# A 480-byte tile at the far end of the right side of SBUF, ahead of every other tile there

## The chip, the cores and the metric

The kernel runs on one core of one Trainium2 chip. The metric is the device time in microseconds of one execution. A profile of one execution of the kernel before is there as well; its "span" runs from the first to the last instruction on the core.

## The reference

Three layers run one after the other, all in float32, on 1,536 tokens (2 batches of 768) of width 512:

```
attention: 8 heads of 64; each query sees the keys less than 16 positions away,
           and 24 block summaries (max of k, mean of v over 32 tokens)
moe:       a token with x @ w_skip > 0 is computed, the others pass;
           its expert e = argmax(x @ w_gate) of 8;  x += gate * relu(x @ w1[e]) @ w2[e]
           w1 is 8 x 512 x 1024, w2 is 8 x 1024 x 512
moe2:      out = (sigmoid(x @ w_gate) * (x @ w_val)) @ w_out,   512 -> 1536 -> 512, float64 weights
```

The third layer's weights arrive as 64-bit words; the kernel makes float32 values of them and splits each into a high part of type fp32r, on which TensorE runs in one pass, and a low part that holds the rest.

## The kernel before

**Stages.** Attention fills the first 80 us: 12 tiles of 128 tokens, whose operations stand in an order that a planner worked out ahead from written costs. Each tile's result goes to a DRAM tile x_d. The MoE stage runs to about 200 us: 64 tiles of weights (512 KB each) and four tiles of raw weights of the third layer stream in through three rings of buffers, SP issuing every load; eight experts run one after the other on TensorE (`e_s1` L731, `e_s2_mm` L764, plain float32). POOL gathers tokens from x_d by index (L709, L1010) and adds results back into x_d by index (L787, L895). These adds and gathers follow one another, since each waits for the one that last wrote x_d. For experts with many tokens `o_tile` runs a second tile with split weights (`mm`, L860). In this execution it ran twice. The rest, from about 200 us, is the third layer.

**The third layer.** d_ff = 1536 is cut into six groups g of 256 columns, the tokens into three parts c of 512. A unit u = 3g + c does for one group and one part:

- `m_s1(u, f)` for f = 0, 1: for gate and value, four blocks n of the width, three matmuls each, 24 in all, 48 in a unit (L1175);
- `m_gate`: sigmoid on ACT, product on DVE, its high part on ACT, its low part on DVE (L1187 to L1191);
- `m_s2(u - 1, r)` for r = 0 to 3, one unit later: six matmuls each, 24 in all (L1204), and the sum in ACC on DVE (L1210, L1212).

```
for a, b in ((hi, XH), (hi, XL), (lo, XH)):
    x = b[c][n] if c == 0 else b[c][:, n, :]
    pe.matmul(ps, a[:, o:o + 128], x, start=k == 0, stop=k == 11)        # L1175: stationary, moving
...
for a, b in ((GH, hi), (GH, lo), (GL, hi)):
    pe.matmul(ps, a[u][:, f, r * 128:r * 128 + 128], b[:, o + a0:o + a1], ...)   # L1204
```

Here hi, lo = WHL[g % 2]. `m2_split` makes the weights of a group out of raw ones (L983 to L997, on DVE, ACT and POOL) while earlier units run. The first two units are broken by transposes of the tokens, `x2` (L1153), which wait for loads of x_d (L1148).

**Where the tiles lie.** A pool stands on the left or on the right side of SBUF. Left pools grow up from the low addresses, right ones down from byte 229,344 of a partition, which is 447 x 512 + 480. The sizes of the pools' large tiles are multiples of 512 bytes. The addresses that the program has before, in bytes of a partition:

| side | tile | first byte | past a multiple of 512 |
|---|---|---|---|
| left | XH[0], XL[0] (eight of 2 KB) and `o_tile`'s split weights | 19,968 to 36,352 | 0 |
| left | WHL[0]: wh0, wl0 | 36,352; 48,640 | 0 |
| left | ring b (loads 25 to 34 of the weights) | 36,352 to 77,312 | 0 |
| right | `o_tile`'s split tokens xoT, hoT | 90,976 to 99,168 | 352 |
| right | xgT, the MoE stage's tokens | 105,312; 107,360 | 352 |
| right | GH, GL (two of each) | 122,848; 126,944; 131,040; 135,136 | 480 |
| right | ACC | 147,424 | 480 |
| right | WHL[1]: wh1, wl1 | 172,000; 184,288 | 480 |
| right | XH[1], XH[2], XL[1], XL[2] | 196,576; 204,768; 212,960; 221,152 | 480 |
| right | rings a and c (the other weights, the raw ones) | 131,040 to 229,344 | 480 |

So in L1175 the stationary operand is left for even g and right for odd g, the moving one left for c = 0 and right for c = 1, 2. In L1204 the stationary operand (GH, GL) is always right and the moving one left for even g, right for odd g. In L860 the stationary operand (xoT, hoT) is right, at 352, the moving one left, at 0.

Of the kernel before, what the change touches and what calls it, by code (L numbers as in the profile page):

```python
# [9 lines left out]
F32 = mybir.dt.float32  # L10
# [141 lines left out]
def body(ctx: ExitStack, tc, qx, kx, vx, vtx, cst, csa, wgs, w1, w2, mgate, mval, mout, out):  # L152
    nc = tc.nc
    pe, dve, act, pool, sp = nc.tensor, nc.vector, nc.scalar, nc.gpsimd, nc.sync
# [20 lines left out]
    MORE = keep.tile([128, E, 12], F32, name="MORE")  # L175
    WIDX = keep.tile([128, NOV], I32, name="WIDX")
    NL = keep.tile([128, 1], I32, name="NL")

    wst = ExitStack()
    wring = wst.enter_context(tc.tile_pool(name="wring", bufs=NWA, side="right"))  # L180
# [266 lines left out]
    def count():  # L447
# [6 lines left out]
        dve.tensor_reduce(NLF, MORE.rearrange("p a b -> p (a b)"), axis=AX, op=ALU.add)  # L454
        dve.tensor_copy(NL, NLF)

# [443 lines left out]
    lp = lst.enter_context(tc.tile_pool(name="lp", bufs=1, side="left"))  # L900
    nl = nc.values_load(NL[0:1, 0:1], min_val=0, max_val=NOV)
    with tc.If(nl > 0):
# [393 lines left out]
```

## Time and profile before

| | |
|---|---|
| median of 3 runs | 512.0 us (511.83 to 513.35) |
| the profiled execution | 514.23 us, span 512.4 us |
| mean granted TensorE clock of the profiled execution | 0.97 of full speed |
| TensorE matmul busy | 491.8 us, 96% of the span |
| VectorE, ScalarE, GpSimd busy | 287.4, 187.3, 108.6 us |
| moved by DMA | 83.08 MB |

A busy time is the time in which an engine had an instruction in flight. Matmuls are pipelined, so the busy time of one is longer than its distance to the next: in the rows below a matmul lasts some 0.39 us and the next starts some 0.23 us after it. The pace is therefore read from a stretch of consecutive matmuls divided by their number.

### The profile page before, as it was taken

What the parts mean: (1) busy time and instruction counts of PE and PEld (TensorE: products, weight loads), DVE (VectorE), ACT (ScalarE), POOL (GpSimd) and SP (SyncE); (2) the same over time, 40 slices, a digit from 0 to 9 for tenths busy, and PEclk for the clock granted to TensorE, in tenths of its full rate; (3) what the DMA queues carried; (4) which work ended last, traced back from release to release, by engine and by line L of the source; (5) the groups of instructions that cost most, each with busy time, mean ns of one, the idle gap of its engine ahead of it and who ended that gap; (6) DMA issues with size and microseconds to landing.
All of it is one profiled execution on the core that took longest, in us unless ns stands there. A gap on an engine that the chain in (4) does not pass through costs nothing.

```text
span 512.4 us, 8115 instructions
## 1 busy us (share of the span) xinstructions
PE 491.8 (96%) x2889; PEld 372.3 (73%) x2889; DVE 287.4 (56%) x813; ACT 187.3 (37%) x403; POOL 108.6 (21%) x157
## 2 busy tenths in 40 slices
PE   6999998899999978899999999999999999999997
PEld 3988884346574535688888888888888888888886
DVE  4889787217481544257855565455646465456324
ACT  2888862017471323234432233223232232222110
POOL 5664223610121221012211121112211221112000
PEclk9799997599999989899999999999999999999999
DMA  8889889999997863742222220122012220000114
GB/s 272 295 247 305 239 285 347 376 349 405 392 399 276 252 202 97 233 187 83 82 82 84 82 83 6 78 82 83 19 64 83 82 83 0 1 0 0 43 41 165
DMA packets 27483, 83.08 MB, mean 162 GB/s; under 512 B 3096, under 2 KB 5016, under 8 KB 25384
## 3 DMA queue, kind: packets, MB, share of 16 engines
q1 hardware_dynamic: 25032, 77.71, 43.1%
q0 software_dynamic: 2400, 4.72, 4.1%
q8 instruction: 28, 0.46, 0.4%
q14 instruction: 23, 0.19, 0.1%
HBM read 73.69 MB, written 8.13 MB: 160 GB/s over the span
## 4 chain that ended last, share of the span: by engine, by line
PE 58%; DMA 8%; issue 2%; SPq 0%; POOLq 0%; DVE 0%
PE s L1175 38%; PE s L1204 19%; DMA x_d<-ysb,SI 6%; PE x2p L1153 1%; DMA xg<-x_d 1%; DMA x2t<-x_d 1%; DMA x_d<-yo,SI 0%; SPq L1100 0%; POOLq L1028 0%; DVE ACC L1212 0%; POOLq L787 0%; SPq L1148 0%; POOLq L997 0%
## 5 line engine op out<-in xcount | busy, mean ns | idle before, releaser
L1175 PE MATMUL s<-XH,wh 128*128 128x512 f32 x288 | 114.1, 396 | 0.0
L1175 PE MATMUL s<-XH,wl 128*128 128x512 f32 x288 | 113.2, 393 | 0.0
L1175 PE MATMUL s<-XL,wh 128*128 128x512 f32 x288 | 113.2, 393 | 0.0
L997 POOL TENSOR_TENSOR wl<-x,wh 128x512 fp32r<-128x512 f32 x32 | 42.1, 1317 | 223.1 <-ACT wh L996 214.4
L1189 DVE TENSOR_TENSOR pr<-s,sg 128x512 f32<-128x512 f32 x36 | 24.9, 691 | 92.6 <-PE s L1175 88.8
L1175 PEld LDWEIGHTS s<-XH,wh 128*128 128x128 f32 x288 | 54.4, 189 | 12.4 <-issue 0.2
L1175 PEld LDWEIGHTS s<-XH,wl 128*128 128x128 f32 x288 | 54.2, 188 | 12.4
L1175 PEld LDWEIGHTS s<-XL,wh 128*128 128x128 f32 x288 | 54.2, 188 | 12.3 <-DVE XL L1128 0.2
L1204 PE MATMUL s<-wh,GL 128*128 128x512 f32 (+1 forms) x146 | 56.8, 389 | 0.0
L1204 PE MATMUL s<-wl,GH 128*128 128x512 f32 (+1 forms) x146 | 56.8, 389 | 0.0
L1204 PE MATMUL s<-wh,GH 128*128 128x512 f32 (+1 forms) x146 | 56.8, 389 | 0.0
L1190 ACT ACTIVATE GH<-pr 128x512 fp32r<-128x512 f32 x36 | 22.8, 632 | 68.0 <-DVE pr L1189 68.0
L996 ACT ACTIVATE wh<-x 128x512 fp32r<-128x512 f32 x36 | 22.7, 632 | 67.2 <-DVE x L990 67.2
L1212 DVE TENSOR_TENSOR ACC<-s,ACC 128x512 f32<-128x512 f32 (+1 forms) x61 | 39.1, 677 | 7.8 <-PE s L1204 7.8
L1191 DVE TENSOR_TENSOR GL<-pr,GH 128x512 fp32r<-128x512 f32 x36 | 24.9, 692 | 25.1 <-ACT GH L1190 25.1
L985 ACT ACTIVATE u<-u 128x512 f32<-128x512 f32 x36 | 22.5, 626 | 43.5 <-DVE u L983 43.5
L731 PE MATMUL hp<-wt,xgT 128*64 128x512 f32 x128 | 33.7, 657 | 0.6 <-ACT xgT L721 0.6
L341 ACT ACTIVATE P<-P,nm 128x120 f32<-128x120 f32 x96 | 29.7, 383 | 5.8 <-DVE nm L334 5.8
L1204 PEld LDWEIGHTS s<-wl,GH 128*128 128x128 f32 x146 | 27.4, 188 | 6.1
L1204 PEld LDWEIGHTS s<-wh,GH 128*128 128x128 f32 x146 | 27.4, 188 | 6.1
L1204 PEld LDWEIGHTS s<-wh,GL 128*128 128x128 f32 x146 | 27.4, 188 | 6.0
L325 PE MATMUL S<-kw,qb 128*128 128x120 f32 x192 | 28.5, 295 | 3.0 <-DVE kw L548 1.8
(185 smaller groups left out, 695.5 us busy)
## 6 DMA issues: line engine op xcount, KB each, us to landing
wt<-w SPq DMA_DIRECT2D x64, 512.0 KB
wr<-mout SPq DMA_DIRECT2D x6, 1024.0 KB
wr<-mgate SPq DMA_DIRECT2D x5, 1024.0 KB
wr<-mval SPq DMA_DIRECT2D x5, 1024.0 KB
vw<-vx SPq DMA_DIRECT2D x12, 390.0 KB
kr<-kx SPq DMA_DIRECT2D x8, 400.0 KB
qs<-qx SPq DMA_DIRECT2D x12, 256.0 KB
vt<-vtx SPq DMA_DIRECT2D x8, 384.0 KB
```

Of the source, the lines that this page charges most:

```text
L325: pe.matmul(Sp[i][:, n, :], qb[t % 3][:, j, n, :], kwb[i % 3][:, n, :], start=True, stop=True)
L341: act.activation(Pt[i][:, n, :], Pt[i][:, n, :], AF.Exp, bias=nmt[i][:, n:n + 1], scale=-1.0)
L731: pe.matmul(hp[e][c * 64:c * 64 + 64, :], xgT[e // 2][:, n, (e % 2) * 64:(e % 2) * 64 + 64], WT[2 * e, n][:, c * 512:c * 512 + 512], start ...
L985: act.activation(u, u, AF.Copy, scale=2.0 ** -112)
L996: act.activation(hi[:, d], w, AF.Copy)
L997: (dve if g == 0 and k < WLE else pool).tensor_tensor(lo[:, d], w, hi[:, d].bitcast(F32), op=ALU.subtract)
L1175: pe.matmul(ps, a[:, o:o + 128], x, start=k == 0, stop=k == 11)
L1189: dve.tensor_tensor(pr, pp[1], sg, op=ALU.mult)
L1190: act.activation(GH[u][:, f, :], pr, AF.Copy)
L1191: dve.tensor_tensor(GL[u][:, f, :], pr, GH[u][:, f, :].bitcast(F32), op=ALU.subtract)
L1204: pe.matmul(ps, a[u][:, f, r * 128:r * 128 + 128], b[:, o + a0:o + a1], start=k == 0, stop=k == 5)
L1212: dve.tensor_tensor(acc, ps, acc, op=ALU.add)
```

## The change

A pool of one tile is opened on the right side before all others there. It is 120 float32 values wide (480 bytes) and stays to the end. POOL clears its first column; nothing reads it. All other tiles of the right side come to lie 480 bytes lower, the left side stays.

```
     NL = keep.tile([128, 1], I32, name="NL")
 
+    edge = ctx.enter_context(tc.tile_pool(name="edge", bufs=1, side="right"))
+    EDGE = edge.tile([128, 120], F32, name="EDGE")
+    pool.memset(EDGE[:, :1], 0.0)
+
     wst = ExitStack()
     wring = wst.enter_context(tc.tile_pool(name="wring", bufs=NWA, side="right"))
```

The right side's large tiles of the third layer and of the rings then stand at 0 past a multiple of 512 (wh1 at 171,520 = 335 x 512), xoT, hoT and xgT at 384. Tiles of attention that stood at an odd multiple of 32 bytes come to an even one, and the other way round.

## Rows read from the trace of the kernel before

**Rows 1.** The page: the span, and busy time by engine.

```profile
span 512.4 us, 8115 instructions
PE 491.8 (96%) x2889; PEld 372.3 (73%) x2889; DVE 287.4 (56%) x813; ACT 187.3 (37%) x403; POOL 108.6 (21%) x157
```

**Rows 2.** Chain that ended last, 212 to 510 us: start, length, what.

```profile
by line: PE s L1175 65.1%; PE s L1204 33.4%; PE x2p L1153 1.2%; DVE ACC L1212 0.1%; issue 0.0%
...
217.01 8.36 PE s L1175 x36
...
229.91 2.80 PE s L1175 x12
232.72 5.60 PE s L1204 x24
238.31 11.20 PE s L1175 x48
...
271.92 10.92 PE s L1175 x48
282.83 5.44 PE s L1204 x24
288.27 10.88 PE s L1175 x48
...
304.60 10.91 PE s L1175 x48
315.51 5.47 PE s L1204 x24
320.99 11.20 PE s L1175 x48
```

**Rows 3.** Windows, L1175 alone: busy, PEclk, DMA share, GB/s.

```profile
255.12:266.31 11.19, 11.19 (x48) 8.65 (x47) 1.00 0.27 94
271.92:282.83 10.91, 10.91 (x48) 8.66 (x47) 1.00 0.19 81
304.60:315.51 10.91, 10.91 (x48) 8.66 (x47) 1.00 0.20 83
320.99:332.18 11.19, 11.19 (x48) 8.67 (x47) 1.00 0.20 83
```

**Rows 4.** Timeline of TensorE in the first o_tile, 119 to 133 us.

```profile
127.48 0.40 PE L860 MATMUL yq<-wh,hoT0l 128*128 128x512 f32 x1
...
132.17 0.39 PE L860 MATMUL yq<-wh,hoT1l 128*128 128x512 f32 x1
```

**Rows 5.** Timeline of POOL, 130 to 212 us: adds into x_d, idle before them.

```profile
133.87 1.59 POOL L895 DMA_INDIRECT x_d<-yo,SI  x1 [11.15 <-DVE yo L894]
142.65 1.67 POOL L787 DMA_INDIRECT x_d<-ysb,SI  x1 [7.20 <-DMA x_d<-yo,SI]
```

**Rows 6.** Chain that ended last, before 212 us.

```profile
166.86 4.30 DMA x_d<-ysb,SI
...
171.91 9.74 DMA x_d<-ysb,SI
...
189.37 3.98 DMA x_d<-ysb,SI
```

**Rows 7.** Timeline of TensorE: L731 with weights right, then left (expert 3).

```profile
113.61 1.94 PE L731 MATMUL hp<-wt,xgT 128*64 128x512 f32 x8
...
134.95 1.94 PE L731 MATMUL hp<-wt,xgT 128*64 128x512 f32 x8
```

**Rows 8.** SP's loads; windows of their stream: busy by engine, PEclk, DMA share, GB/s.

```profile
103.96 30.77 SPq L278 DMA_DIRECT2D wt<-w  x23
135.75 1.53 SPq L278 DMA_DIRECT2D rh<-mgate  x2
...
121.50:126.50 5.00, 4.99 (x24) 3.63 (x22) 4.25 (x8) 4.44 (x9) 1.01 (x1) 1.00 1.02 419
...
142.50:147.30 4.80, 4.80 (x24) 3.87 (x23) 3.78 (x7) 4.15 (x8) 1.67 (x1) 1.00 1.04 422
```

**Rows 9.** Timelines of POOL and TensorE at the start.

```profile
0.33 0.10 POOL L1286 MEMSET const-uint8-127<- 128x1 uint8 x1
0.72 0.52 POOL L530 MEMSET Z<- 128x512 f32 x1 [0.29 <-POOLq L1286]
...
8.15 0.68 PE L325 MATMUL S<-kw,qb 128*128 128x120 f32 x4 [1.01 <-ACT kw L547]
```

**Rows 10.** Window of unit 2: busy on PE, PEld, DVE, ACT, POOL; then POOL's splits.

```profile
238.00:249.50 11.50, 11.50 (x51) 9.27 (x50) 9.79 (x18) 4.06 (x7) 2.32 (x2) 1.00 0.08 13
...
248.47 3.19 POOL L997 TENSOR_TENSOR wl<-x,wh 128x512 fp32r<-128x512 f32 x2 [6.77 <-ACT wh L996]
```

## The prediction

> **What bounds the kernel now.** I read the page first: matmuls are in flight for 96% of the span [rows 1]. The chain of waits then says where that decides. From 212 us to the end the chain is TensorE and nothing else, 65.1% in L1175 and 33.4% in L1204, with no wait between [rows 2]. So in the third layer, nearly 300 of 512 us, the time is the number of matmuls times their pace, and whatever changes the pace comes out at the end in full. Before 212 us the chain is a string of DMAs that add into x_d one after the other [rows 6].
>
> The second reading is the pace itself, from the pieces of that chain. The same 48 matmuls of L1175 take 11.20 us in some units (238.31, 320.99) and 10.88 in others (288.27): 233.3 ns and 226.7 ns each. The 24 of L1204 take 5.60 or 5.44, the same two paces [rows 2]. [...]
>
> What sorts them is where the two operands lie. By the kernel's loop, g is even in units 0 to 2, 6 to 8, 12 to 14:
>
> - L1175, both operands left (unit 6 at 304.60, c = 0, g even): fast. Both right (units 4 and 5 at 271.92 and 288.27): fast.
> - L1175, one left and one right (unit 2 at 238.31, unit 7 at 320.99; unit 3 as well, at 255.12 [rows 3]): slow.
> - L1204, both right (g odd, 282.83): fast; stationary right, moving left (g even, 232.72, 332.18 and seven more): slow.
>
> The units not shown, up to 17, repeat this. Left tiles start at a multiple of 512 bytes, right ones 480 past one. So "one left, one right" is also "the two start 480 bytes apart in that count", and "same side" is "0 apart". After a change of sides the first dozen matmuls still run between the paces, which is why 271.92 has 10.92 and not 10.88 [rows 2].
>
> **The change part by part.** (1) *Third layer.* After the change left and right tiles all start at a multiple of 512. If the distance of the operands sets the pace, every unit has what both-left units have now (0 and 0), which is fast. What goes, from the chain's pieces against 10.88 and 5.44: eight L1175 units of 11.19 to 11.20 (units 2, 3, 7, 8, 9, 13, 14, 15), 8 x 0.32 = 2.53 us with the hundredths; nine L1204 pieces of 5.60, 9 x 0.16 = 1.44; five units of 10.91 and 10.92 and four of 5.45 and 5.47, 0.26 together; units 0 and 1, which transposes break up, 36 matmuls in 8.36 instead of 36 x 0.2267 = 8.16, and two dozens in 2.80 instead of 2.72, 0.36. Sum 4.59 [rows 2]. The four transposes' breaks stay and leave some uneven matmuls behind them; I take 4.5. Bounds: 0 if the side and not the distance is what counts; 4.6 above.
>
> (2) *o_tile.* L860 has its stationary operand at 352 and its moving one at 0. It runs at (132.17 - 127.48) / 20 = 234.5 ns, slow too [rows 4]. This speaks against the mere distance in bytes: these tiles lie 55 to 79 KB from their moving ones and are slow, GH and GL 33 to 74 KB from wh1 and wl1 and fast. After the change it stands at 384 against 0; no row has that distance. If that is as good as 0, some 43 matmuls of the first tile save 0.008 each, 0.33 us. VectorE, which makes the split weights, is busy 4.25 of 5.00 us there [rows 8], so it can follow. The add of this tile's result is issued at 133.87 right after DVE, and the next add, 142.65, waits for it [rows 5]; from there the chain of adds runs to 212 us, so the 0.33 could come through whole. The second tile's saving falls beside that chain and is worth nothing. Bounds 0 to 0.33; I take 0.15, as 384 is unseen.
>
> (3) *Other matmuls.* Plain float32 ones don't show the two paces: L731 takes 1.94 us per eight with weights on the right (expert 2, 128 bytes from xgT) and on the left (expert 3, 352) [rows 7]. So moving the tiles of attention and of the experts costs and gives nothing on TensorE; the cover for a hundredth either way is the chain of adds.
>
> (4) *DMA.* The weight rings a and c come to multiples of 512, ring b is there already. Loads land in order of issue: ring b's, the 25th to 34th, are the 4th to 13th of the 23 issued from 103.96 on, the raw ones, which lie right, are issued from 135.75, and both arrive some 6 us later. The rate is 419 GB/s in a window of the former and 422 in one of the latter [rows 8]. So 0 from this. [...]
>
> (5) *The clear.* One more POOL memset ahead of Z. A one-column memset takes 0.10 us [rows 9]. It shifts the warm-up matmuls, whose end is followed by 1.01 us of waiting for ACT [rows 9]: hidden, and 0.1 us if that cover went.
>
> (6) *What is next.* A unit and its L1204 piece come to 16.32 us. In unit 2 DVE is busy 9.79 of 11.50 us and POOL ends the splits for unit 3 at 251.66 [rows 10], 3.4 us ahead of their use at 255.12 [rows 3]. TensorE is about 1 us earlier by then, so the splits are still in time. DVE has less to do later.
>
> Sum: 4.5 + 0.15 = 4.65 us. The profiled execution had 514.23 us with a span of 512.4; the span would be 507.75. The runs' median is 512.0, 2.2 under the profiled execution's time; the same saving gives 507.35, say 507.4.
>
> **The rivals.** *(B) Nothing changes: 512.0.* The pace goes with the side, by some part of SBUF, and not with the distance modulo 512. For it: before, the two can't be parted in the third layer. Against it: L860, whose distances overlap the fast ones, and that both-left and both-right pairs have one pace to within 1 ns. [...]
>
> *(D) Part of the gain is given back: 508.8.* DVE, 85% busy in unit 2 [rows 10], becomes the bound in units 1 to 3, while it makes the second group's weights. Then their 3 x (0.32 + 0.16) = 1.4 us don't come. Against it: 3.4 us of margin.
>
> *(C) Slower.* TensorE's 0.3 us in the o_tiles move the last weight loads, issued from 168 us on, against the adds into x_d. An add took 9.74 us among those loads and 4.30 or 3.98 outside [rows 6], each on the chain. One more such add costs 5.44: 507.35 + 5.44 = 512.8, still the same; two cost 5.44 + 5.76: 518.5, slower. It decides only from the second on, and needs both of them among the loads.
>
> [...]
>
> **How the numbers follow.** The forecast (all units fast, 506.2 to 508.4) has 0.75, D 0.08, B 0.11, C 0.04 (half of it in each of its two ends), E 0.02. The range 505.9 to 510.0 holds the forecast with repeats and D, and leaves out B, C and E, under 2 in 10. Faster by over 0.3%, about what a measurement of this kernel can tell, means under 510.5: 0.75 + 0.08 + 0.02 = 0.85. Same 0.11 + 0.02 = 0.13; slower 0.02.
>
> **What would show it.** All L1175 pieces of the chain from unit 2 on at 10.88 and all L1204 ones at 5.44, with no second level; L860 at 227 ns or at 234 tells whether 384 counts as 0; L731 at 1.94; the weight stream at 420 GB/s; the add at 133.87 earlier by up to 0.33 us. The prediction is wrong if units with one operand on each side stay at 11.20 (B), if they all go to 11.20, or if 212 us, where the third layer's chain begins, moves by more than a few tenths.

## The result, and the profile after

The changed kernel has a median of 507.17 us (11 runs, 504.0 to 510.82) against 513.35 (11 runs, 509.51 to 514.7) for the kernel before. The ratio is 0.990, interval 0.9869 to 0.9932: faster by 0.7 to 1.3%. A later series of 12 more runs gave 507.68 and a ratio of 0.9916, interval 0.9885 to 0.9947. The profiled execution took 510.82 us, span 509.0 us.

Line numbers from L179 on are four higher than before. The page of the changed kernel, span and busy time, as in [rows 1]:

```profile
span 509.0 us, 8116 instructions
PE 486.7 (96%) x2889; PEld 371.7 (73%) x2889; DVE 287.2 (56%) x813; ACT 187.2 (37%) x403; POOL 107.8 (21%) x158
```

The chain that ended last, changed kernel, third layer, as in [rows 2] (start, length, what):

```profile
211.84 1.90 PE x2p L1157 x8
213.74 3.56 PE s L1179 x12
...
218.17 8.18 PE s L1179 x36
...
230.84 2.74 PE s L1179 x12
233.57 5.44 PE s L1208 x24
239.01 10.88 PE s L1179 x48
...
255.33 10.88 PE s L1179 x48
...
271.65 10.88 PE s L1179 x48
...
320.61 10.88 PE s L1179 x48
331.49 5.44 PE s L1208 x24
...
505.68 0.42 DVE ACC L1216
```

The second level is gone. The units at 239.01 (unit 2, one operand on each side), 255.33 (unit 3, the sides exchanged) and 320.61 (unit 7) now take what unit 4 at 271.65 takes. The piece that had 10.92 at a change of sides has 10.88 as well. The windows say the same at the same clock, 1.00, and with much the same transfers beside them as in [rows 3]:

```profile
255.33:266.21 10.88, 10.88 (x48) 8.67 (x47) 1.00 0.28 96
...
320.61:331.49 10.88, 10.88 (x48) 8.66 (x47) 1.00 0.21 86
```

The end of the chain before, for the sum that follows:

```profile
509.06 0.42 DVE ACC L1212
```

From unit 2's L1175 to the last sum in ACC the profile before has 509.06 - 238.31 = 270.75 us, the one after 505.68 - 239.01 = 266.67: 4.08 less. Units 0 and 1 give 0.18 (36 matmuls, 8.18 instead of 8.36), 0.12 (the two dozens) and 0.16 (the first L1204 piece). Together 4.54 us.

This leaves out the dozen of unit 0 between the first two sets of transposes, at 213.74, whose operands both lie left in both kernels. It took 3.56 us after and 3.32 before, and from the first transposes to the end the third layer is 4.34 us shorter. In 213.40 to 215.30 us of the profile after, the granted clock was 0.50; TensorE had waited 2.28 us for tokens just before. In the traces of the experiments below the dozen takes from 2.74 us (E5) to 4.32 (E7), and the wait alone doesn't set it: before, TensorE had waited longer, 2.44 us, and the dozen was shorter.

The rest of the rows are about what they were. The extra expert tile, timeline of TensorE as in [rows 4]:

```profile
128.41 0.39 PE L864 MATMUL yq<-wh,hoT0l 128*128 128x512 f32 x1
...
133.06 0.40 PE L864 MATMUL yq<-wh,hoT1l 128*128 128x512 f32 x1
```

The adds into x_d, POOL's timeline as in [rows 5], then the chain before 212 us as in [rows 6]:

```profile
134.77 1.59 POOL L899 DMA_INDIRECT x_d<-yo,SI  x1 [11.69 <-DVE yo L898]
```

```profile
168.60 8.05 DMA x_d<-ysb,SI
...
177.39 7.08 DMA x_d<-ysb,SI
...
185.21 4.33 DMA x_d<-ysb,SI
...
190.27 3.83 DMA x_d<-ysb,SI
```

The stream of weights in the two windows of [rows 8], and POOL's start as in [rows 9]:

```profile
121.50:126.50 5.00, 5.00 (x25) 4.10 (x24) 4.00 (x7) 4.39 (x8) 1.00 (x1) 1.00 1.03 420
142.50:147.30 4.80, 4.80 (x22) 3.83 (x21) 3.80 (x7) 3.65 (x8) 1.82 (x1) 1.00 1.03 421
```

```profile
0.72 0.10 POOL L181 MEMSET EDGE<- 128x1 f32 x1 [0.29 <-POOLq L1290]
...
0.76 0.52 POOL L534 MEMSET Z<- 128x512 f32 x1
```

In this profile the third layer starts 0.96 us later than before (211.84 against 210.88) and is 4.34 us shorter, so the spans differ by only 3.4 us. Whether that delay belongs to the change is asked below.

### The profile page after: what moved, and what is told of

Read it like the earlier page. It is cut to its first block, busy times and chain, and to the rows that moved or that the text cites. A ratio compares the mean times of both kernels' runs of the same rounds, so it can differ in the third digit from the quotient of the medians.

```text
span 509.0 us, 8116 instructions
## 1 busy us (share of the span) xinstructions
PE 486.7 (96%) x2889; PEld 371.7 (73%) x2889; DVE 287.2 (56%) x813; ACT 187.2 (37%) x403; POOL 107.8 (21%) x158
## 4 chain that ended last, share of the span: by engine, by line
PE 58%; DMA 8%; issue 2%; SPq 0%; POOLq 0%; DVE 0%
PE s L1179 38%; PE s L1208 19%; DMA x_d<-ysb,SI 6%; PE x2p L1157 1%; DMA xg<-x_d 1%; DMA x2t<-x_d 1%; DMA x_d<-yo,SI 0%; SPq L1104 0%; POOLq L1032 0%; DVE ACC L1216 0%; POOLq L791 0%; SPq L1152 0%; POOLq L1001 0%
## 5 line engine op out<-in xcount | busy, mean ns | idle before, releaser
L1191 ACT ACTIVATE sg<-s 128x512 f32<-128x512 f32 x36 | 21.1, 587 | 26.0 <-PE s L1179 26.0
## 6 DMA issues: line engine op xcount, KB each, us to landing
wt<-w SPq DMA_DIRECT2D x64, 512.0 KB, 11.3
```

Source lines behind the costliest of these rows:

```text
L1191: act.activation(sg, pp[0], AF.Sigmoid)
```

## The experiments

Two theories of the gain stood against each other: the *distance* theory (the pace goes with how far apart the two operands start, modulo some number of bytes, which I took to be 512) and its rivals (the side of SBUF as such; the boundary as such; any move of the right side, or the extra memset).

**E1: the same tile, 512 bytes long.** Everything on the right moves, the distance stays 480.

```
-    EDGE = edge.tile([128, 120], F32, name="EDGE")
+    EDGE = edge.tile([128, 128], F32, name="EDGE")
```

> The tile at the far end is 512 bytes instead of 480: the same extra memset, the same move of every right-hand tile, but the distance between left and right tiles is 480 past a multiple of 512 as before. Distance theory (the pace goes with the distance of the two operands modulo 512): two paces as before, 11.20 and 10.88 us per 48 matmuls in the same units, third layer 4.6 us longer than with 480 bytes, time as before within its spread (ratio to before 0.995 to 1.005). Rival (moving the right side or the extra tile helps in itself): all units 10.88 us, ratio about 0.99.

Measured: 512.92 us (10 runs), ratio to before 0.9985, interval 0.9958 to 1.0012. Its chain:

```profile
238.56 11.19 PE s L1179 x48
249.75 5.60 PE s L1208 x24
255.34 11.20 PE s L1179 x48
...
288.50 10.88 PE s L1179 x48
```

Both paces are back, each in its old units (unit 5 at 288.50 has both operands on the right). So neither the memset nor the move as such changes the paces, and the time shows nothing of them either, within the interval.

**E2: the 480 bytes on the left.** No 512-byte boundary on either side, distance 0.

```
     NL = keep.tile([128, 1], I32, name="NL")
+    EDGE = keep.tile([128, 120], F32, name="EDGE")
+    pool.memset(EDGE[:, :1], 0.0)
```

(The right-hand pool is left out.)

> The 480-byte tile goes to the left side, behind the small tiles that stay: left and right large tiles all start 480 bytes past a multiple of 512, none on a 512-byte boundary. Distance theory: all units of the third layer at 10.88 and 5.44 us, ratio to before about 0.99, as with the change. Rival (it is the boundary that counts): with both sides off it, no unit gains over before, 11.20 in the same units, or all units fall to 11.20; ratio 1.00 or above.

Measured: 508.11 us (4 runs), ratio 0.9898, interval 0.9853 to 0.9944. Its chain:

```profile
238.61 10.88 PE s L1178 x48
249.49 5.44 PE s L1207 x24
254.93 10.88 PE s L1178 x48
```

All are fast with every large tile 480 past a boundary. The boundary is not what counts; that the two sides agree is.

**E3, E5, E6, E7: other distances.** One number of the change, the tile's width, set to 88, 112, 104 and 56 values.

```
-    EDGE = edge.tile([128, 120], F32, name="EDGE")
+    EDGE = edge.tile([128, 88], F32, name="EDGE")     # E5: 112, E6: 104, E7: 56
```

> The tile at the far end is 352 bytes: right-hand tiles of the third layer stand 128 bytes past a multiple of 512, the left ones at 0; the split tokens of the extra expert tiles come to 0, as their moving operands have it. Distance theory: units with one operand on each side slow, at 232 to 233 ns per matmul (128 bytes off was 232 ns in the extra expert tiles after the change), and the matmuls of the extra expert tiles (L860 before) at 226.7 ns for the first time. Rival (128 bytes is as good as 0, 64 or 128 being the step that counts): all units at 226.7 ns. Rival for the extra tiles (something else holds them at 232): they stay at 232 to 235 ns.

> [...] Distance theory in the form that any distance other than 0 modulo 512 is slow: mixed units at 232 to 233.3 ns, same-side units at 226.7. Rival (the pace falls off gradually with the distance, 128 bytes having given 232.4 and 480 233.3): mixed units well under 232, near 228.

> The tile is 416 bytes: 64 bytes apart. Distance modulo 512: mixed units slow, 232 to 233.3 ns. Rival (only whether both start at an even or odd multiple of 32 bytes counts, and 128 was slow for another reason): 226.7 in mixed units.

> The tile is 224 bytes: 256 bytes apart. Distance modulo 512: mixed units slow, 232 to 233.3 ns, and the time that of before. Rival (the step that counts is 256 bytes): mixed units at 226.7 ns as with the change, and a tile of 224 bytes would have done as much as one of 480.

Measured, some of the pieces in the chain; unit 2 is the first piece of 48 in each. E3 (128 bytes apart; 509.95 us in one run):

```profile
228.95 5.58 PE s L1208 x24
234.53 11.14 PE s L1179 x48
...
251.26 11.20 PE s L1179 x48
```

Its extra expert tile, timeline of TensorE as in [rows 4]:

```profile
127.29 0.39 PE L864 MATMUL yq<-wh,hoT1h 128*128 128x512 f32 x1
...
129.56 0.39 PE L864 MATMUL yq<-wh,hoT1l 128*128 128x512 f32 x1
```

E5 (32 apart; 512.65 us in one run):

```profile
236.77 11.20 PE s L1179 x48
247.97 5.60 PE s L1208 x24
```

E6 (64 apart; 512.1 us in one run):

```profile
231.25 5.60 PE s L1208 x24
236.86 11.00 PE s L1179 x48
...
335.88 11.20 PE s L1179 x48
```

E7 (256 apart; 507.98 us in one run, 511.85 in one run for the kernel before in the same series):

```profile
236.18 10.88 PE s L1179 x48
247.06 5.44 PE s L1208 x24
252.50 10.88 PE s L1179 x48
```

E5 agrees with the distance theory: 32 bytes, the smallest distance tried, cost as much as 480. E7 refutes it in the form that I had: 256 bytes apart is as good as 0, so the step is 256 and not 512, and for the third layer a tile of 224 bytes does what the one of 480 does. (The 480 of before is then 224 modulo 256.) E3 and E6 lie between. 128 apart gives 232 ns (11.14 / 48) in unit 2, with the stationary operand left and the moving one right, but 233.3 in unit 3 (251.26), where it is the other way round. 64 apart gives 229.2 ns in unit 2 and 233.3 in unit 8 (335.88), which use the same tiles. So a distance that is no multiple of 256 doesn't fix one pace. What else decides, no run here shows.

E3's second expectation came too: its split tokens stand at 0, as their moving operands do, and ten of the extra expert tile's matmuls take 129.56 - 127.29 = 2.27 us, 227 ns each.

**E4: the extra expert tiles as well.** 384 bytes ahead of the expert stage's tiles, so that xoT and hoT start at 0 past a multiple of 512, as their moving operands do.

```
+    PAD = m1.tile([128, 96], F32, name="PAD")
     xg = [m1.tile([128, DM], F32, name=f"xg{j}") for j in range(4)]
```

> The change kept, and 384 bytes more ahead of the expert stage's tiles, so that the split tokens of the extra expert tiles stand at 0 past a multiple of 512 too, not at 384. Distance theory: their matmuls go from 232 to 226.7 ns, some 40 x 5.5 = 0.2 us less in each of the two tiles; the time is that of the change within its spread, at best 0.2 us less, since the first tile alone is ahead of the chain of adds. Rival (VectorE's split weights or the break by transposes set that pace): 232 ns stays.

Measured: 507.44 us (10 runs), ratio to before 0.9897, interval 0.9863 to 0.9932. TensorE's timeline in the first tile:

```profile
126.90 0.39 PE L865 MATMUL yq<-wl,hoT1h 128*128 128x512 f32 x1
...
129.17 0.39 PE L865 MATMUL yq<-wh,hoT1l 128*128 128x512 f32 x1
```

Ten matmuls in 2.27 us: 227 ns, against 234.5 before and (133.06 - 128.41) / 20 = 232.5 with the change. With E3 that makes two kernels in which these matmuls reach 227 ns at distance 0, so they follow the distance too, and VectorE keeps up: in neither timeline does one of the ten wait. The tile's 48 matmuls, first start to last, take 12.50 us before, 12.42 with the change, 12.30 here and 12.25 in E3.

**E8: one pair parted within the right side.** The change, and 32 bytes between two right-hand pools, so that only GH and GL move.

```
+    zp = ctx.enter_context(tc.tile_pool(name="zp", bufs=1, side="right"))
+    PAD = zp.tile([128, 8], F32, name="PAD")
     z2 = ctx.enter_context(tc.tile_pool(name="z2", bufs=2, side="right"))
```

> The change kept, and a 32-byte tile between two right-hand pools, so that GH and GL alone stand 32 bytes off: their matmuls (the 24 per unit) then have operands 32 bytes apart on the right side for odd groups and 480 apart across the sides for even ones. Distance theory: all 24s at 5.60 us, those with both operands right too, all 48s at 10.88; third layer 18 x 0.16 = 2.9 us longer than with the change. Side theory (a pair on one side is fast whatever its distance): the 24s of odd groups stay at 5.44, only those of even groups go to 5.60.

Measured: 509.04 us in one run. Its chain:

```profile
234.57 10.89 PE s L1181 x48
...
261.93 5.59 PE s L1210 x24
267.53 10.89 PE s L1181 x48
278.41 5.59 PE s L1210 x24
284.01 10.89 PE s L1181 x48
...
503.91 0.42 DVE ACC L1218
```

The piece at 278.41 is unit 3's second product, GH with wh1 and wl1, both on the right: 5.59, where it had 5.44. The pieces of the first product stay fast. From unit 2 to the end it takes 503.91 - 234.57 = 269.34 us, 2.67 more than with the change; 17 x 0.16 = 2.7 was to be expected from there on. That leaves nothing for the side as such.

**E9 and E10: E4's kernel and the change alone, in one longer series.**

> The change with the extra expert tiles' operands aligned as well, timed longer beside the change alone. Distance theory: 0.1 to 0.2 us less than the change alone at best, which the spread of the runs (some 5 us) hides: ratio between the two within 0.997 to 1.003. Rival (the earlier add of the first extra tile starts the whole chain of adds on a better footing, as the early start of the third layer at 208 us in one profile could suggest): 2 to 3 us less than the change alone.

> The change alone once more, in the same series: 4.5 us less than before, ratio 0.988 to 0.994, and all units at 10.88 and 5.44 us. The start of the third layer in its profile, 211.8 us the first time, falls anywhere between 208 and 213 if it is chance.

Measured: E9 507.71 us (7 runs), ratio to before 0.9899, interval 0.9863 to 0.9935; E10 507.68 us (12 runs), 0.9916, interval 0.9885 to 0.9947. The two can't be told apart, so E4's 0.1 to 0.2 us stays a reading of the traces. No version measurably better than the change came out of this.

**The start of the third layer.** In the two profiles of the change its first transposes start at 211.84 and (E10) 210.54 us, in the two of E4's kernel at 208.08 and (E9) 210.71, in E1's at 210.83, in E2's at 212.90, before at 210.88. So one program differs by 1.3 us and another by 2.6 from one execution to the next, and before's 210.88 lies between the two of the change. Most of a difference stands there before the chain of adds: the add of the first extra tile was issued at 133.87 before and 134.77 after, 0.90 of the 0.96 us, and at 130.87 in E4 and 133.28 in E9, 2.41 of the 2.63. The single adds differ too (4.30, 9.74, 6.25, 3.98 us before, 8.05, 7.08, 4.33, 3.83 after), but the four together take 24.27 and 23.29 us.

## Why the prediction was right, and where it was not

**The third layer, 4.5 us: right.** It is 4.54 from the pieces of the chain that I had summed. All steps of that part held: the sorting by operands, the level that the mixed units fall to, and the sum over them. I had named both-left units of before as the state that all units were to get, but took the level of 10.88 from a both-right one (288.27); both-left ones read 10.91, with their uneven start. After the change every unit from 2 on has 10.88. The dozen of unit 0 between the transposes, which my sum left out, took 0.24 us back in this profile.

**The time, 507.4 us: closer than the parts deserve.** The measured 507.17 is within 0.3 us of the forecast, but that is partly luck. I subtracted 4.65 from a median of 512.0 over three runs; the kernel before then measured 513.35, so the medians differ by 6.18 us, where the ratio of 0.990 means 5.1 and the later series' 0.9916 means 4.3. The two intervals come to 3.5 to 6.7 and 2.7 to 5.9 us: both hold what the traces show, 4.54 and the 0.08 of the extra tile, and neither is narrow enough to confirm it. What the medians show beyond that lies within the spread.

**"Modulo 512": the step that was wrong.** Where I wrote that the distance "in that count" of 512 sets the pace, E7 shows that 256 is the step. Before, every large pair was 0 or 480 apart, so the trace could not part the two, and I took the number from the tiles' sizes. For this change it makes no difference, 0 being a multiple of both.

**o_tile, 0.15 us: too large.** The condition "If that is as good as 0" did not hold: 384 is 128 modulo 256, and L860 went from 234.5 to 232.5 ns only. The first tile became 0.08 us shorter. Its add came not earlier but 0.90 us later, since the tile itself began 0.97 later (120.64 against 119.67). My upper bound was too high as well: with aligned operands the first tile saves 0.20 us (E4) or 0.25 (E3), not 0.33, since the pace of 227 ns comes only some matmuls after the tile's start and after its transposes: in E4 ten matmuls take 2.33 us from 117.21 on, 233 ns each, and the next eight 1.81, 226 ns; behind the last transposes seven take 1.61 us from 124.61 on, 230 ns, and the next thirteen 2.95, 227 ns. That either amount reaches the end I argued from the chain of adds; the spread of that chain hides it.

**Other matmuls, DMA, the clear: as written, the first on too little.** L731's eight matmuls take 1.94 us on either side of the change. They also have two records each in the trace before, 128 for the 64 of the kernel, where an fp32r matmul has one, 864 for the 18 x 48 of L1175, which is what the trace shows of its one pass. But [rows 7] could not show that plain float32 is free of the two paces: neither of its distances, 128 and 352, is a multiple of 256, and the 384 of after isn't one either. E4 settles it, where xgT and the weights stand 0 apart and the same eight take as long:

```profile
131.94 1.94 PE L736 MATMUL hp<-wt,xgT 128*64 128x512 f32 x8
```

The stream runs at 420 and 421 GB/s in the windows that had 419 and 422: raw weights that moved from 480 to 0 past 512 load no faster. The memset puts Z's clear 0.04 us later.

**The rivals.** B is refuted by the result and, for the side as such, by E8. The clock and the transfers are no reason for the two paces either: before, the clock was 1.00 at both, and the DMA share 0.20 at 10.91 us (304.60) and at 11.19 (320.99) [rows 3]. E, faster right-hand loads, did not come: no run shows the gain that its chance of 0.02 stands on; in its place the runs show 420 and 421 GB/s where there were 419 and 422. D did not come: unit 3, which uses the splits made last, took 10.88 us without a wait. C did not come in the form I gave. But what runs before the third layer is less steady than I assumed: I wrote that a move of the 212 us by more than a few tenths would speak against the prediction, and it moved 0.96 later in one profile and 0.34 earlier in the next. As one program moves by 1.3 to 2.6 us between its own two profiles, that sign was no use; a shift of some tenths by the change would not be seen among them.

**What stays open:** why these fp32r matmuls take 226.7 ns with operands a multiple of 256 bytes apart and 233.3 with 32 or 480, why 64 and 128 bytes apart give more than one pace, and why the plain float32 matmuls show none of it.

## What to carry to other kernels

When the same fp32r matmul has two paces at one clock, sort its instances by the addresses of both operands before looking for a wait: here 3% of the pace, 226.7 or 233.3 ns, hung on whether they started a multiple of 256 bytes apart. Large tiles on the two sides of SBUF agreed here only once both ends started alike; a filler at one end (224 bytes would have done, 10.88 us per 48 matmuls in E7) set all pairs of large tiles at once, and it was the agreement that counted, on a boundary or not (10.88 us with the change and in E2). Inspect each pool for its own remainder: a filler at the far end leaves the pools behind small odd-sized tiles where they fall (here xoT and hoT at 384, 232.5 ns).

## What was not expected of the hardware

That the loss does not grow with the distance: 32 bytes apart cost the full 6.7 ns on top of 226.7 (E5), as 480 did, and 64 and 128 cost less in some units (229.2 and 232 ns in unit 2 of E6 and E3). That the pace does not change at once: after a change from one kind of pair to the other it took some ten matmuls to settle (before, nine take 2.08 us from 271.75 on, 231 ns each, and the next thirteen 2.95, 227 ns), which is the 10.92 instead of 10.88 at 271.92 in [rows 2]. That with 64 bytes between the operands two units with the same tiles ran at 229.2 and 233.3 ns (E6). And that the plain float32 matmuls of the experts show none of it (1.94 us per eight at distances of 128 and 352 bytes before, 384 after and 0 in E4).
